# Linear attention with a gated product: q's last 64 tokens in float32r parts, attention in 288-column halves

## The chip, the core and the metric

The kernel runs on one core of a Trainium2 chip. The metric is device time in microseconds, from the start to the end of one execution. The engines are PE (TensorE, matmuls), DVE (VectorE), ACT (ScalarE), POOL (GpSimd) and SP (SyncE, which issues the DMAs here); each runs its own list of instructions in order and waits on semaphores for the others.

## The reference

Eight batches, eight heads, 576 tokens, 64 channels a head; q, k and v in float32. First linear attention, then a gated product:

```python
q_s = softmax(q over the 64 channels)            # exp(q - max), divided by sum + 1e-9
k_s = softmax(k over the 576 tokens)
kv = einsum('bhsd,bhse->bhde', k_s, v)           # 64 x 64 per head
x = einsum('bhsd,bhde->bhse', q_s, kv)           # then (batch, token, 512 channels)

gate = sigmoid(causal convolution of x over tokens, 5 taps, one weight per tap and channel)
val = x @ w_val                                  # 512 x 512
out = (gate * val) @ w_out                       # 512 x 512
```

The three weights arrive as float64. The kernel reads them as pairs of 32-bit words and builds float32 values of them on the chip.

## The kernel before, in words

**Layout.** From the attention on, everything is kept with channels on the partitions: a batch is four blocks of 128 channels (two heads each) by 576 tokens. Tokens are split into 512 "main" ones, in four groups of 128, and a tail of 64; the tails of an even and the following odd batch share one tile of 128 rows.

**Products in parts.** A float32 matmul runs as two instructions on PE, a high and a low pass. To avoid that, the two large products (`value` and `project`, by `split_product`, L528) split both sides into a float32r high part and a float32r rest, and add up three matmuls: low weight with high data, high with high, high with low. Each is done for the two halves of the 576 tokens, 288 columns, which lie in two PSUM banks side by side (`halved_bank`, L544). One `value` or `project` of a 128-channel block is so 4 x 3 x 2 = 24 matmuls.

**Attention** (`attend`, L481) takes one channel block of one batch. In batches 2 to 7 (not in `F32_BATCHES`, L25) it multiplies kv's parts (`kvs`, made by `kv_high` and `kv_low`) with q's parts for the 512 main tokens, three float32r matmuls of 512 columns, and then does the tail's 64 tokens with one float32 matmul from `kvd` (kv in float32) and `qTt` (the tail of q, turned). Batches 0 and 1 use float32 for all of it. q reaches this layout through PE: `q_turn` (L454) transposes eight 128 x 128 pieces into PSUM, `q_turned` copies them as the high part `qT`, `q_low` (L465, DVE) subtracts that from PSUM for the rest `qTlo`; `tail_turn` and `tail_turned` do the tail of two batches at once, in float32.

**After attention** x stays in PSUM while seven steps read it: `x_high` (a float32r copy, L497), `x_low` (the rest, DVE, L509), `first` (the last tap, L501), and four `tap`s (L513). A tap on DVE (`v`) is one multiply-add into the gate tile; a tap on ACT (`a`) writes a scaled copy `far`, which POOL then adds. Then `sigmoid` (ACT), `value` (PE), `gated` (DVE, value times gate), `g_high` (a float32r copy) and `g_low` (the rest, POOL or DVE), `project` (PE), `store` (a copy from PSUM and a DMA).

**Before it** come, per batch, for k: loads of a strided copy, `k_peak` (the maximum over tokens, DVE), `k_row` and `k_spread` (the row of maxima to DRAM and back, spread over the partitions), `k_sub` (five subtractions), `k_exp`; for q: `q_max`, `q_sub`, `q_exp`, `q_sum`, `q_mul`. Batches 0 and 1 have shorter ways through PE (`k_top`, `k_raise`, `k_turn`; for batch 0 `q_lift`, `q_peak`, `q_top`, `q_minus`, `q_raise`). The weights come in eight slabs (`load_words` 0 to 7; 8 is the convolution): `field`, `scaled`, `signed`, `part`, `joined` build a float32 value, `w_high` and `w_low` its parts.

**Order.** All of it stands in one list written out by hand, `ORDER` (L32 to L135), some 900 steps such as `tap 3 1 2 v`: batch 3, block 1, tap 2, on DVE. A letter chooses the engine (`a` ACT, `v` DVE, `p` POOL). Each engine does its own steps in the order of the list, and waits where the list puts a step ahead of its inputs.

**Buffers that the change touches.** PSUM has two buffers called "x" (attention, q's transposes, and the peaks and sums of the start) and two called "mm" (products, kv, the other transposes). The parts of x have six buffers each, `xh` and `xl`. One ring called `words`, four buffers of 4 KB a partition, holds the raw weight words, kv's parts and q's low parts. `qT` and `qTt` have one buffer each.

Of the kernel before, what the change touches and what calls it, by code (L numbers as in the profile page):

```python
# [24 lines left out]
F32_BATCHES = (0, 1)  # L25
# [17 lines left out]
    load_words 4, field 4, q_turned 0 0 a, signed 0, q_turned 0 1 a, scaled 2 a, q_sum 1, w_high 3 v, q_mul 0 4 p,
    joined 0 p, part 2 a, tail_turn 0, load_q 2, tail_turned 0 a, load_k 3, signed 2, attend 0 1, k_raise 1 2,
    first 0 1 a, x_high 0 1 a, load_v 1, field 5, tap 0 1 3 v, tap 0 1 2 v, tap 0 1 1 v, k_raise 1 0, joined 2 p,
    k_raise 1 3, attend 0 0, k_tail_turn 1, w_low 3 p, warm 8, first 0 0 a, x_low 0 1, x_high 0 0 a, tap 0 1 0 v,
    k_turn 1 0, w_high 0 a, k_tail_turned 1 a, tap 0 0 3 v, q_mul 1 3 p, x_low 0 0, scaled 5 a, k_turn 1 1,
    tap 0 0 2 v, load_v 4, tap 0 0 1 v, k_turned 1 0 a, part 4 a, q_mul 1 2 p, k_turned 1 1 a, scaled 4 a, attend 0 2,
    kv 1, q_mul 1 1 p, load_words 7, signed 4, w_low 0 p, first 0 2 a, tap 0 0 0 v, attend 0 3, part 5 a,
    load_words 6, x_high 0 2 a, sigmoid 0 0, tap 0 2 3 v, load_v 2, w_high 2 a, x_high 0 3 a, signed 5, x_low 0 2,  # L50
    first 0 3 a, kv_norm 1 a, joined 4 p, tap 0 2 2 v, joined 5 p, w_low 2 p, q_mul 1 0 p, x_low 0 3, load_km 2 1,
    w_high 4 a, tap 0 3 3 v, value 0 0, gated 0 0, tap 0 2 1 v, tap 0 3 2 v, field 7, w_low 4 p, w_high 5 a,
# [596 lines left out]
```

## Time and profile before

| | us |
|---|---|
| median of 3 runs (lowest to highest) | 320.44 (319.13 to 321.22) |
| the profiled execution | 321.3 |
| its span in the trace | 319.5 |

| engine | busy us of the span | share | instructions |
|---|---|---|---|
| PE, matmuls | 299.5 | 94% | 2553 |
| DVE | 268.2 | 84% | 363 |
| ACT | 203.4 | 64% | 315 |
| POOL | 187.8 | 59% | 156 |

Busy time of PE is modelled for pipelined matmuls: an instruction counts until its result has left the array, while the next has already begun, so start-to-start times are the safer measure of what a run of matmuls costs. An engine's idle time costs something only where it is on the way to the end. The mean granted TensorE clock was 0.998 of full speed. The `project` and `value` matmuls take 42% of the chain that ended last, attention's 4%.

### The profile page before, as it was taken

What the parts mean: (1) busy time and instruction counts of PE and PEld (TensorE: products, weight loads), DVE (VectorE), ACT (ScalarE), POOL (GpSimd) and SP (SyncE); (2) the same over time, 40 slices, a digit from 0 to 9 for tenths busy, and PEclk for the clock granted to TensorE, in tenths of its full rate; (3) what the DMA queues carried; (4) which work ended last, traced back from release to release, by engine and by line L of the source; (5) the groups of instructions that cost most, each with busy time, mean ns of one, the idle gap of its engine ahead of it and who ended that gap; (6) DMA issues with size and microseconds to landing.
All of it is one profiled execution on the core that took longest, in us unless ns stands there. A gap on an engine that the chain in (4) does not pass through costs nothing.

```text
span 319.5 us, 6403 instructions
## 1 busy us (share of the span) xinstructions
PE 299.5 (94%) x2553; PEld 276.4 (87%) x2553; DVE 268.2 (84%) x363; ACT 203.4 (64%) x315; POOL 187.8 (59%) x156
## 2 busy tenths in 40 slices
PE   2998689989899979999999999999999999999996
PEld 1347469988799969989999999999999999999995
DVE  3769999997897999799996979899899989868530
ACT  1579998665968499747983887569643773432200
POOL 2174467799867748858686776665758353311500
PEclk9999999999999999999999999999999999999999
DMA  7994897614798154663428178409300120012013
GB/s 247 376 388 153 301 400 272 201 37 147 237 248 312 50 172 174 193 249 98 147 56 327 42 242 260 182 0 353 99 0 25 50 77 0 2 74 76 0 39 111
DMA packets 20525, 51.25 MB, mean 160 GB/s; under 512 B 2832, under 2 KB 7312, under 8 KB 17808
## 3 DMA queue, kind: packets, MB, share of 16 engines
q1 hardware_dynamic: 20496, 50.85, 45.9%
q8 instruction: 20, 0.33, 0.5%
q14 instruction: 9, 0.07, 0.1%
HBM read 41.39 MB, written 9.45 MB: 159 GB/s over the span
## 4 chain that ended last, share of the span: by engine, by line
PE 60%; DMA 13%; ACT 12%; DVE 9%; issue 3%; POOL 2%; SPq 1%; DVEq 0%; POOLq 0%; ACTq 0%
PE val L535 21%; PE out L535 21%; DMA km<-in_k_strided 4%; PE kv L426 4%; PE x L491 4%; PE qTps L458 3%; DMA out<-o 2%; PE qlps L404 2%; DMA q<-in_q 2%; DVE gate L517 2%; PE qlps L409 2%; DMA kmax<-krow 2%; ACT far L520 2%; DVE kpk L273 2%; DMA ident<-in_ident 1%
## 5 line engine op out<-in xcount | busy, mean ns | idle before, releaser
L517 DVE SCALAR_TENSOR_TENSOR gate<-x,cw,gate 128x575 f32<-128x575 f32 (+3 forms) x99 | 78.1, 808 | 3.3 <-POOL gate L521 1.5
L521 POOL TENSOR_TENSOR gate<-gate,far 128x572 f32<-128x572 f32 (+3 forms) x29 | 39.6, 1369 | 39.0 <-ACT far L520 38.7
L535 PE MATMUL out<-gh,w_out_lo 128*128 128x288 f32 x256 | 56.9, 301 | 0.5 <-ACT gh L159 0.5
L535 PE MATMUL val<-xh,w_val_lo 128*128 128x288 f32 x256 | 56.5, 302 | 0.8 <-DVE o L161 0.7
L535 PE MATMUL out<-gl,w_out_hi 128*128 128x288 f32 x256 | 55.6, 296 | 0.9 <-DVE gl L564 0.9
L535 PE MATMUL val<-xl,w_val_hi 128*128 128x288 f32 x256 | 55.0, 296 | 0.8 <-DVE xl L511 0.8
L535 PE MATMUL out<-gh,w_out_hi 128*128 128x288 f32 x256 | 55.5, 295 | 0.0
L535 PE MATMUL val<-xh,w_val_hi 128*128 128x288 f32 x256 | 54.8, 295 | 0.0
L564 POOL TENSOR_TENSOR gl<-g,gh 128x576 fp32r<-128x576 f32 x25 | 36.5, 1463 | 30.5 <-ACT gh L159 23.3
L535 PEld LDWEIGHTS out<-gl,w_out_hi 128*128 128x128 f32 x256 | 41.4, 188 | 1.3 <-DVE gl L564 1.3
L535 PEld LDWEIGHTS val<-xh,w_val_lo 128*128 128x128 f32 x256 | 40.9, 188 | 1.6 <-DVE o L161 0.9
L535 PEld LDWEIGHTS val<-xl,w_val_hi 128*128 128x128 f32 x256 | 41.3, 188 | 1.0 <-DVE xl L511 1.0
L535 PEld LDWEIGHTS out<-gh,w_out_lo 128*128 128x128 f32 x256 | 41.2, 189 | 0.8 <-ACT gh L159 0.8
L535 PEld LDWEIGHTS out<-gh,w_out_hi 128*128 128x128 f32 x256 | 41.6, 188 | 0.0
L535 PEld LDWEIGHTS val<-xh,w_val_hi 128*128 128x128 f32 x256 | 41.3, 188 | 0.0
L382 POOL TENSOR_TENSOR q<-q,qs 128x512 f32<-128x512 f32 x25 | 26.2, 1068 | 16.3 <-DVE qs L362 16.3
L556 DVE TENSOR_TENSOR g<-val,gate 128x576 f32<-128x576 f32 x32 | 23.9, 751 | 9.8 <-PE val L535 6.9
L520 ACT ACTIVATE far<-x,cw 128x572 f32<-128x572 f32 (+3 forms) x29 | 21.0, 738 | 14.2 <-DVE gate L517 9.3
L159 ACT CAST gh<-g 128x576 fp32r<-128x576 f32 x25 | 16.8, 671 | 18.2 <-DVE g L556 18.2
L159 ACT COPY o<-out 128x576 f32<-128x576 f32 (+1 forms) x22 | 13.5, 617 | 21.9 <-PE out L535 12.1
L288 POOL TENSOR_TENSOR k<-k,kmax 128x512 f32<-128x512 f32 x18 | 25.0, 1402 | 1.3 <-DMA kmax<-krow 1.3
L524 ACT ACTIVATE gate<-gate 128x576 f32<-128x576 f32 x32 | 21.6, 685 | 6.0 <-DVE gate L517 3.5
(101 smaller groups left out, 588.0 us busy)
## 6 DMA issues: line engine op xcount, KB each, us to landing
out<-o SPq DMA_DIRECT2D x31, 288.0 KB, 2.3
...
```

What stands on the lines that cost most here:

```text
L159: nc.scalar.copy(out=out, in_=in_)
L288: engine(e).tensor_sub(kk[r, cs], kk[r, cs], mx[r, cs])
L382: engine(e).tensor_mul(qq, qq, s.unsqueeze(2).broadcast_to([P, H, D]))
L426: nc.tensor.matmul(acc[h * D:(h + 1) * D, p, :], T["k", b][:, c, cs] if c < 4 else ktz[b % 2][:, cs], T["v", b][:, c, hd] if c < 4 else T[ ...
L491: nc.tensor.matmul(ps[:, :MAIN], a, z, start=(i == 0), stop=(i == len(parts) - 1))
L517: nc.vector.scalar_tensor_tensor(out=a, in0=x, scalar=w, in1=a, op0=ALU.mult, op1=ALU.add)
L520: nc.scalar.activation(part, x, AF.Copy, scale=w)
L521: nc.gpsimd.tensor_add(a, a, part)
L524: nc.scalar.activation(T["gate", b, p], T["gate", b, p], AF.Sigmoid)
L535: nc.tensor.matmul(ps[:, cs], a[:, kb, ms], z[kb][:, cs], start=(kb == 0 and i == 0), stop=(kb == NB - 1 and i == 2),)
L556: nc.vector.tensor_mul(T["g", b, m], T["val", b, m], T["gate", b, m])
L564: engine(e).tensor_sub(T["gl", b, m], T["g", b, m], T["gh", b, m].bitcast(F32))
```

## The change

- Batch 1 leaves `F32_BATCHES`: its attention is done with parts, as batches 2 to 7 are. That adds `kv_high`, `kv_low` and two `q_low` for it.
- q's tail gets parts too. `qT` and `qTlo` grow from 512 to 576 columns a block; `tail_high` copies the batch's 64 tail columns of all four blocks from `qTt` into `qT` as float32r, `tail_low` subtracts that for two blocks at a time into `qTlo`. The float32 matmul of the tail goes.
- `attend` writes into a halved bank, and each of its matmuls is done for the two halves of 288 columns: six matmuls a step (four in batch 0, whose single float32 product is halved too).
- `xh` and `xl` become the two halves of one tile, six buffers called "pair". The weight words take buffers of the same ring. Kv's parts get a ring of their own with one buffer, q's low parts one with two.
- `ORDER` is new throughout, with other choices of engine.

```diff
-F32_BATCHES = (0, 1)
+F32_BATCHES = (0,)
...
+    def pair(name, dtype):
+        return work.tile([P, 2 * S], dtype, tag="pair", name=name, bufs=6)
...
-            T["words", i] = small.tile([P, n, 2], I32, tag="words", name=f"words{i}", bufs=4)
+            T["words", i] = pair(f"words{i}", I32)[:, :2 * C].rearrange("p (n t) -> p n t", t=2)
...
-        t = T["kvs", b] = small.tile([P, 2, C], F32R, tag="words", name=f"kvs_{b}", bufs=4)
+        t = T["kvs", b] = small.tile([P, 2, C], F32R, tag="kvs", name=f"kvs_{b}", bufs=1)
...
+    def q_across(b):
+        if ("qT", b) not in T:
+            T["qT", b] = work.tile([P, NB, S], F32 if b in F32_BATCHES else F32R, tag="qT", name=f"qT_{b}")
+        return T["qT", b]
...
+    def q_under(b, g):
+        if ("qTlo", b, g) not in T:
+            T["qTlo", b, g] = small.tile([P, 2, S], F32R, tag="qTlo", name=f"qTlo_{b}_{g}", bufs=2)
+        return T["qTlo", b, g]
...
+    def tail_high(b, e="p"):
+        copied(e, q_across(b)[:, :, MAIN:], T["qTt", b][:, :, rows(b)])
+
+    def tail_low(b, g, e="p"):
+        ps = slice(2 * g, 2 * g + 2)
+        engine(e).tensor_sub(q_under(b, g)[:, :, MAIN:], T["qTt", b][:, ps, rows(b)], T["qT", b][:, ps, MAIN:].bitcast(F32))
+
     def attend(b, p):
 
-        ps = bank(f"x_{b}_{p}", "x")
+        T["x", b, p] = halved_bank(f"x_{b}_{p}", "x")
...
         for i, (a, z) in enumerate(parts):
-            nc.tensor.matmul(ps[:, :MAIN], a, z, start=(i == 0), stop=(i == len(parts) - 1))
-        nc.tensor.matmul(ps[:, MAIN:S], kvd[b % 2][:, p], T["qTt", b][:, p, rows(b)], start=True, stop=True)
-        T["x", b, p] = ps[:, :S]
+            for cs in tokens("a"):
+                nc.tensor.matmul(T["x", b, p][:, cs], a, z[:, cs], start=(i == 0), stop=(i == len(parts) - 1))
...
-        xh = T["xh", b, p] = block("xh", f"xh_{b}_{p}", 6, F32R)
+        T["xx", b, p] = pair(f"x2_{b}_{p}", F32R)
+        xh = T["xh", b, p] = T["xx", b, p][:, :S]
...
-        xl = T["xl", b, p] = block("xl", f"xl_{b}_{p}", 6, F32R)
+        xl = T["xl", b, p] = T["xx", b, p][:, S:]
```

Of the new order, its beginning, and the places in batches 2, 3 and 4 that the prediction follows:

```diff
+    load_kc 0 1, load_q 0 0 2, k_top 0 1, load_kc 0 0, q_max 0 0 2, load_ident, q_peak 0 0 2, load_words 8, k_top 0 0,
+    load_words 1, field 1, q_top 0 0 2 a, scaled 1 v, load_q 0 2 5, field 8, signed 1, load_words 3, q_max 0 2 5,
+    load_kc 0 2, q_lift 0 0, k_raise 0 0, q_minus 0 0, load_kc 1 1, load_kc 0 3, q_peak 0 2 5, k_raise 0 1,
+    scaled 8 v, load_q 1, q_top 0 2 5 a, signed 8, field 3, part 3 v, k_top 1 1, part 1 p, scaled 3 a, k_top 0 2,
+    k_raise 1 1, warm 0, joined 1 p, warm 0, k_turn 0 0, load_kc 1 2, signed 3, q_raise 0 0, w_high 1 p, q_lift 0 1,
...
+    tap 2 1 1 v, k_sub 3 4 p, tap 2 1 0 v, project 1 1, k_sub 3 3 p, load_v 4, q_exp 3, q_sum 3, attend 2 2,
+    tap 2 0 1 a, q_mul 3 0 p, load_km 6 0, tap 2 0 0 a, x_high 2 2 v, k_peak 4 2, store 1 3 a, attend 2 3, load_q 4,
...
+    gated 2 0, q_sub 4 4 p, q_turned 3 0 v, g_high 2 1 a, value 2 2, kv_low 3 p, q_low 3 0, q_turned 3 1 a, q_low 3 1,
+    attend 3 0, value 2 3, x_high 3 0 a, first 3 0 a, q_sub 4 3 p, g_high 2 0 p, load_km 5 3, g_low 2 0 v,
+    g_low 2 1 p, gated 2 2, tap 3 0 3 v, k_peak 5 0, gated 2 3, g_high 2 2 p, x_low 3 0, g_high 2 3 v, load_km 5 2,
+    g_low 2 3 v, q_sub 4 1 p, load_q 5, g_low 2 2 p, k_sub 4 1 p, k_peak 5 2, q_sub 4 2 p, tail_low 3 1 p,
+    k_sub 4 0 p, attend 3 1, load_km 6 1, first 3 1 a, tap 3 0 2 a, tap 3 0 1 a, project 2 0, x_high 3 1 a,
...
+    q_turned 4 1 a, k_sub 5 3 v, k_peak 6 1, value 3 3, q_low 4 0, kv_low 4 v, tail_high 4 v, g_low 3 1 v, gated 3 2,
+    k_sub 5 1 p, k_peak 6 3, load_v 6, tail_low 4 0 v, g_low 3 0 p, q_low 4 1, attend 4 0, g_high 3 2 a, gated 3 3,
```

The steps of the old order that stand against the start:

```diff
-    load_kc 0 1, load_q 0 0 2, load_words 8, k_top 0 1, load_ident, q_lift 0 0, q_max 0 0 2, q_peak 0 0 2,
-    load_kc 0 0, k_top 0 0, load_words 1, load_kc 0 3, load_q 0 2 5, field 1, q_top 0 0 2 v, field 8, load_words 3,
-    q_minus 0 0, scaled 1 a, k_raise 0 1, k_top 0 3, part 1 a, k_raise 0 0, signed 1, load_kc 0 2, scaled 8 a,
-    q_max 0 2 5, load_kc 1 1, joined 1 p, field 3, load_q 1, q_raise 0 0, signed 8, load_words 0, k_turn 0 0,
...
-    part 3 a, w_low 1 p, k_turned 0 0 a, q_lift 0 1, q_top 0 2 5 a, q_minus 0 1, k_raise 1 1, signed 3, k_raise 0 2,
```

The steps whose engine changes, counted over both lists (before to after): tap on DVE 99 to 89, on ACT and POOL 29 to 39; g_high ACT 25 to 19, DVE 7 to 5, POOL 0 to 8; g_low POOL 25 to 16, DVE 7 to 16; q_sub POOL 22 to 26, DVE 5 to 1; q_mul POOL 25 to 28, DVE 7 to 3, ACT 4 to 5; w_high POOL 0 to 3; tail_high (new) ACT 3, DVE 1, POOL 4; tail_low (new) DVE 3, POOL 11; q_low DVE 12 to 14.

More of the change, by code (lines that the diff above doesn't have):

```diff
@@ L43 @@
[L43 to L52, printed above, removed]
@@ L68 @@
-    tap 1 3 0 v, g_low 1 1 v, sigmoid 1 2, value 1 2, gated 1 2, load_km 4 0, warm 0, tail_turn 2, kv_high 2 a,
-    q_turn 2 0, k_sub 3 0 v, k_peak 4 0, tail_turned 2 a, sigmoid 1 3, q_turn 2 1, load_v 3, q_turned 2 0 a,
-    g_low 1 0 p, g_high 1 2 a, q_turned 2 1 a, q_low 2 0, k_sub 3 4 p, load_q 3, kv_low 2 p, g_low 1 2 p, value 1 3,
-    attend 2 1, q_low 2 1, attend 2 0, x_high 2 1 a, gated 1 3, q_max 3, first 2 1 a, g_high 1 3 a, first 2 0 a,
-    k_sub 3 1 p, load_km 4 2, tap 2 0 3 v, x_low 2 1, tap 2 0 2 v, g_low 1 3 p, q_sub 3 3 p, q_sub 3 0 p, project 1 0,
@@ L93 @@
-    kv_high 4 v, value 3 2, q_turned 4 0 a, tail_turned 4 a, kv_low 4 p, value 3 3, q_sub 5 3 p, q_turned 4 1 a,
-    g_low 3 0 p, k_peak 6 1, sigmoid 3 3, q_low 4 0, gated 3 2, q_low 4 1, attend 4 0, gated 3 3, first 4 0 a,
-    attend 4 1, load_km 7 3, g_high 3 2 v, load_q 6, x_high 4 0 a, g_high 3 3 v, g_low 3 2 p, first 4 1 v, q_exp 5,
-    load_k 6, g_low 3 3 p, tap 4 1 3 a, tap 4 0 3 v, x_low 4 0, project 3 2, tap 4 1 2 a, tap 4 0 2 v, x_high 4 1 a,
-    project 3 1, tap 4 0 1 v, k_sub 5 2 p, tap 4 0 0 v, q_max 6, attend 4 2, x_low 4 1, k_peak 6 2, store 3 2 a,
@@ new lines @@
+    g_low 0 0 p, load_km 2 3, q_low 1 1, gated 0 2, q_low 1 0, kv_low 1 p, g_high 0 1 a, tail_low 1 0 p, g_high 0 2 a,
+    q_sub 2 1 p, g_low 0 2 v, field 6, gated 0 3, k_peak 2 0, part 7 a, attend 1 0, scaled 6 a, signed 6, first 1 0 a,
+    g_high 0 3 a, attend 1 1, g_low 0 3 v, g_low 0 1 p, k_peak 2 3, part 6 a, tap 1 0 3 v, project 0 0,
+    tail_low 1 1 p, q_sub 2 3 p, first 1 1 a, project 0 1, load_km 3 0, joined 7 p, joined 6 p, k_row 2, w_high 7 a,
+    x_high 1 1 a, w_high 6 p, x_high 1 0 a, store 0 0 a, tap 1 1 3 v, x_low 1 1, tap 1 0 2 v, w_low 6 p, tap 1 1 2 v,
@@ new lines @@
+    q_turned 5 0 v, kv_low 5 v, tail_low 5 0 v, q_turn 5 1, q_turned 5 1 a, value 4 3, q_low 5 0, q_low 5 1,
+    attend 5 1, gated 4 2, k_sub 6 3 v, tail_low 5 1 p, sigmoid 4 3, g_low 4 1 p, g_high 4 2 v, first 5 1 a,
+    load_km 7 3, attend 5 0, gated 4 3, g_high 4 3 a, first 5 0 a, tap 5 1 3 v, g_low 4 3 v, tap 5 0 3 v, g_low 4 2 p,
+    project 4 0, tap 5 0 2 v, project 4 1, tap 5 1 2 a, k_peak 7 3, tap 5 1 1 a, x_high 5 1 a, tap 5 1 0 a, x_low 5 1,
+    store 4 0 v, x_high 5 0 a, x_low 5 0, tap 5 0 1 v, sigmoid 5 1, q_sub 6 4 p, attend 5 3, first 5 3 a, project 4 2,
@@ new lines @@
+    value 5 2, q_sub 7 0 v, q_mul 6 0 a, kv_high 6 a, q_mul 6 3 p, g_high 5 1 p, tail_turn 6, q_turn 6 0, q_turn 6 1,
+    sigmoid 5 3, k_peak 7 2, q_turned 6 0 a, g_low 5 1 p, tail_turned 6 v, tail_high 6 p, kv_low 6 p, g_low 5 0 v,
+    q_turned 6 1 a, q_low 6 0, tail_low 6 0 p, q_sub 7 3 p, q_low 6 1, gated 5 2, tail_low 6 1 v, value 5 3,
+    attend 6 1, first 6 1 a, attend 6 0, k_row 7, g_high 5 2 p, gated 5 3, k_spread 7, tap 6 1 3 v, g_low 5 2 v,
+    g_high 5 3 a, x_high 6 0 a, g_low 5 3 v, first 6 0 v, tap 6 1 2 a, project 5 3, x_low 6 0, project 5 0,
```

167 lines of the change are left out of this document (82 added, 85 removed).

## The prediction

> **What bounds the kernel now.** I read the busy times by stretch first, cut where PE begins the first value product of batch 0 (47.4), of batch 2 (121.8), of batch 3 (154.3) and of batch 7 (290.6), and where it ends its last matmul (316.4). Columns: length, then busy time (count) of PE, weight loads, DVE, ACT, POOL, then clock, DMA share, GB/s.
> ```profile
> 0.00:47.40 47.40, 35.95 (x278) 21.58 (x278) 37.06 (x57) 35.05 (x65) 22.28 (x26) 1.00 0.85 310
> 47.40:121.80 74.40, 70.18 (x620) 65.93 (x618) 67.45 (x88) 55.54 (x93) 57.70 (x46) 1.00 0.59 193
> 121.80:154.30 32.50, 31.86 (x230) 30.64 (x229) 30.34 (x38) 24.18 (x39) 24.09 (x20) 1.00 0.49 164
> 154.30:290.60 136.30, 135.82 (x1243) 132.75 (x1242) 120.74 (x166) 83.55 (x114) 78.02 (x62) 1.00 0.32 113
> 290.60:316.40 25.80, 25.73 (x194) 25.49 (x192) 12.66 (x18) 4.75 (x9) 5.72 (x4) 1.00 0.11 41
> ...
> sum 319.50, PE 299.55 PEld 276.39 DVE 268.24 ACT 203.43 POOL 187.80; mean PE 49.92 PEld 46.07 DVE 44.71 ACT 33.91 POOL 31.30
> ```
> PE idles 11.4 us before 47.4, 4.2 in the second stretch, 0.6, 0.5 and 0.1 in the next three, so 5.4 us after 47.4. From 121.8 to the end PE is the bound; every matmul microsecond removed there should come off. Before 47.4 the chain changes from engine to engine. Between 47.4 and 121.8 PE and DVE (67.45 of 74.40) run neck and neck, and a DMA chain joins in, shown below.
>
> **The attention matmuls.** A busy PE overstates pipelined matmuls, so I take start-to-start times from the chain that ended last (start, length, what). Batch 7 first, then two runs of products for the unit price.
> ```profile
> 165.71 6.40 PE val L535 x48
> ...
> 274.20 0.70 PE x L491 x3
> 274.89 0.17 PE x L492 x2
> 275.06 0.74 PE x L491 x3
> 275.80 0.17 PE x L492 x2
> 275.97 6.46 PE out L535 x48
> ...
> 290.75 12.80 PE val L535 x96
> ```
> One 288-column float32r matmul costs 12.80 / 96 = 0.133 us. Two attention steps cost 275.97 - 274.20 = 1.77, and the product behind them is 0.06 longer than its like (6.46 against 6.40), which I put down to the return from float32: 1.83 a pair. After the change an attention step is six 288-column matmuls of the very form of the products: 6 x 0.133 = 0.80, 1.60 a pair. Gain 0.23 a pair, 0.115 a step; batches 2 to 7 have 24 steps: **-2.8 us**. The 64-column float32 matmuls go, two a step (one instruction each for the high and the low pass).
>
> The Trainium skill, "TensorE: Matmul & The Clock Gate", section "Back-to-back issue gap", speaks against this: it gives about 81 ns for a weight load with a 128-column matmul and 131 ns with 512 columns, a mostly fixed price. Interpolated, six at 102 ns would be 0.61 us where three at 131 and two at 81 or less were 0.55, so by that page the halves would lose 0.06 us a step, an estimate. This trace does not agree: 0.133 us at 288 columns and 0.70 / 3 = 0.233 at 512, in proportion to the columns.
>
> Batch 1 goes from float32 to parts. Its attention, in the timeline of PE:
> ```profile
> 62.45 1.02 PE L491 MATMUL x<-qT,kvd 128*128 128x512 f32 x2
> ...
> 63.48 1.08 PE L491 MATMUL x<-qT,kvd 128*128 128x512 f32 x2
> ...
> 64.53 0.51 PE L535 MATMUL out<-gh,w_out_lo 128*128 128x288 f32 x2
> ```
> A pair costs 64.53 - 62.45 = 2.08, with the same 0.06 2.14; after, 1.60. Two pairs: **-1.1**. Batch 0 keeps float32, in halves, four matmuls a step; 576 columns at the same price per column change it by under 0.1 us: 0. Together **-3.9 us** of PE work.
>
> **What the parts cost the other engines.** Rows by group (line, engine, operation, shapes, count | busy, mean ns | idle before):
> ```profile
> L517 DVE SCALAR_TENSOR_TENSOR gate<-x,cw,gate 128x575 f32<-128x575 f32 (+3 forms) x99 | 78.1, 808 | 3.3 <-POOL gate L521 1.5 <-ACT xh L159 0.5 <-ACT gate L505 0.2
> L521 POOL TENSOR_TENSOR gate<-gate,far 128x572 f32<-128x572 f32 (+3 forms) x29 | 39.6, 1369 | 39.0 <-ACT far L520 38.7
> L564 POOL TENSOR_TENSOR gl<-g,gh 128x576 fp32r<-128x576 f32 x25 | 36.5, 1463 | 30.5 <-ACT gh L159 23.3 <-DVE gh L161 7.2
> L288 POOL TENSOR_TENSOR k<-k,kmax 128x512 f32<-128x512 f32 x18 | 25.0, 1402 | 1.3 <-DMA kmax<-krow 1.3
> L556 DVE TENSOR_TENSOR g<-val,gate 128x576 f32<-128x576 f32 x32 | 23.9, 751 | 9.8 <-PE val L535 6.9 <-ACT gate L524 1.4 <-POOL q L349 1.3
> L349 POOL TENSOR_TENSOR q<-q,qm 128x512 f32<-128x512 f32 x22 | 23.3, 1073 | 3.4 <-DVE qm L345 3.4
> L468 DVE TENSOR_TENSOR qTlo<-qTps,qT 128x1024 fp32r<-128x1024 f32 x12 | 14.4, 1217 | 0.6 <-ACT qT L159 0.5
> L524 ACT ACT_TABLE_LOAD x8 | 10.3, 1283 | 0.9 <-DVE gate L517 0.7
> L564 DVE TENSOR_TENSOR gl<-g,gh 128x576 fp32r<-128x576 f32 x7 | 7.0, 1007 | 0.1
> ...
> L253 POOL TENSOR_TENSOR f<-e,f 128x512 int32<-128x512 int32 x8 | 11.1, 1385 | 18.6 <-DVE e L249 14.7 <-ACT xh L159 1.5 <-ACT w_val_hi L159 1.2
> ...
> L253 POOL TENSOR_TENSOR cw<-e,f 128x20 int32<-128x20 int32 x1 | 0.2, 226 | 0.4 <-ACT f L165 0.4
> ```
> I counted the steps of both orders by engine. **DVE**: 10 taps go (-8.1), 9 subtractions of g come (+9.1), 2 of batch 1's q_low (+2.4); of the rest 14 leave and 15 come, of like lengths, which I call even. Net +3.4, about +1.3% of its busy time. **POOL**: 10 tap additions (+13.7), 9 subtractions of g less (-13.2), 4 q_sub and 3 q_mul more (1.07 each, +7.5), and work this trace doesn't show there: 8 copies of g, 3 of weights, 4 tail_high, 11 tail_low. The two L253 rows give 2.36 ns a column, so a 128-column tail_low is 0.48 and a 256-column tail_high 0.78; a copy of g or of weights lies between 0.23 (the shortest row) and 1.46 (the subtraction of that size); I take the middle, 0.85. That is 5.3 + 3.1 + 9.4, and with single steps some **+28 us** (bounds +21 to +35). **ACT**: its 10 more taps replace copies of like size; the new order goes to and fro between exponential and sigmoid 19 times, not 15: 4 table loads, +5.1.
>
> What hides this: POOL idles 132 us of the span, ACT 116, so they cost 0, as long as no matmul waits for the instruction in question; a tap on ACT and POOL lasts 2.1 us where one on DVE lasts 0.8, and what is behind a waiting POOL instruction waits too. DVE's cover is thin only between 47.4 and 121.8: 7 us of idle. Counted by means, its steps from batch 0's first value to batch 2's go from 68.2 to 70.9, while PE's fall from 68.1 to 66.5. I take 0 for it and keep +2.5 as its upper bound.
>
> **New waits.** Attend now needs tail_low, mostly on POOL, and engines take their steps in the order listed. At one place that costs PE time. Between value 2 2 and attend 3 1 (batch 2's third product, batch 3's second attention) PE has attend 3 0 and value 2 3 to do, 0.80 + 3.20 = 4.0 us. POOL has, from the end of value 2 2 on: g_high 2 2, which needs gated 2 2 on DVE, then q_sub 4 1, g_low 2 2, k_sub 4 1, q_sub 4 2, and only then tail_low 3 1. By the rows, 0.75 + 0.85 + 1.07 + 1.46 + 1.40 + 1.07 + 0.48 = 7.1 us. So PE stands 3.1 us before attend 3 1, and project 2 0 is queued behind it. The stretch's present idle of 0.6 falls into it, I take it: **+2.5 us**. Bounds: +1.9 with the shortest copy; and if POOL is busy without a break from kv_low 3 on, as the listing suggests (q_sub 4 3, g_high 2 0 and g_low 2 1 stand in between, and gated 2 2 stands behind a g_low 2 0 that waits for POOL), PE loses 2.3 us more: +4.8. Elsewhere I found the tail's parts at most a us or two late, and take 0: between value 3 3 and attend 4 0 DVE has 5.0 us listed against PE's 3.2.
>
> Tail_high must wait for the last attend of the batch before, since qT has one buffer; it stands behind it: 0. One buffer for kv's parts and two for q's low parts are no wait either: kv_high and q_low of a batch stand behind the last attend of the batch before. The x tile shared by both parts is released by the same products as before: 0. The weight words now share the ring of x tiles: x parts of batch 0 wait for the part and signed steps of words 1, 3, 4 and 5, which stand ahead of them: 0.
>
> **The start.** Up to value 0 0 the order is new throughout. Rows of the chain, then of ACT and DVE:
> ```profile
> 14.40 1.90 PE kps L317 x8
> 16.30 0.64 PE qpk L388 x3
> 16.94 2.29 PE qlps L404 x4
> ```
> ```profile
> L310 ACT ACTIVATE kc<-kc,ktop 128x576 f32<-128x576 f32 x8 | 5.9, 773 | 0.0
> L165 ACT ACTIVATE e<-e 128x512 f32<-128x512 f32 x7 | 4.4, 633 | 3.0 <-DVE e L239 3.0
> L413 ACT ACTIVATE q<-qlps 128x1024 f32<-128x1024 f32 x2 | 2.0, 1023 | 4.6 <-PE qlps L409 4.6
> ```
> ```profile
> 17.33 0.46 ACT L159 COPY qtop<-qpk 8x384 f32<-8x384 f32 x1
> ...
> 49.58 0.75 DVE L511 TENSOR_TENSOR xl<-x,xh 128x576 fp32r<-128x576 f32 x1
> ```
> The identity now follows a 288 KB load in place of a 20 KB one (about 0.9 us at 310 GB/s), but the peaks are turned before q is lifted, so the copy of the peaks no longer holds PE between: even, so the first subtraction still ends at 14.4. Then PE turns three peaks (0.64, to 15.0) and ACT does q_top 0 2 5, scaled 3, k_raise 1 1 and only then q_raise 0 0: 0.46 + 0.63 + 0.77 + 1.02 = 2.9, to 17.9. q_lift 0 1 needs that PSUM bank and started at 16.94. So +1.0, which passes to the last q_raise and the sum on DVE. From there to the last xl of batch 0 (ends at 50.3) DVE's steps add up to the same in both orders (25.8 and 25.9 us), and PE's value 0 0 ends on it. **+1.0 us**, bounds -1 (the new interleaving gains on DVE) and +2.5 (q's fourth part on POOL is late, behind the new steps there).
>
> **The q chain of batch 3**, which ends in PE's longest wait after 47.4:
> ```profile
> 97.44 6.94 DMA q<-in_q
> 104.41 2.29 DVE qm L345
> ...
> 113.25 0.72 ACT far L520
> ```
> ```profile
> PE x L491 <- ACT far L520: 1.8, 1, 1.8
> ```
> The load of q waits for the turn of batch 2's q, then q_max, subtractions, q_exp and a far tap that must read x before attend 2 3 may overwrite it. The new order has the same chain, with two far taps behind q_exp where one was (+0.7), but attend 2 2 is moved in front of the wait (0.8 of PE work, which then fills it). 0.
>
> **Sum.** -2.8 - 1.1 + 2.5 + 1.0 = **-0.4 us**. The profiled run took 321.3 (span 319.5 and 1.8 around it), 0.9 above the median of 320.44; so 320.9 beside it, and **320.0 us** as a median. A measurement of this kernel tells about 1% (3.2 us) from no change: 317.2 and 323.6 are the lines.
>
> **Rivals.**
> 1. *Faster: the order closes gaps.* The start does not lose its 1.0, and of the 4.2 us that PE idles between 47.4 and 121.8 three quarters go: 320.0 - 4.2 = 315.8. For it: 10 taps leave DVE, whose taps and x parts are what attention waits for there, and every other term is -3.9. Against: the causes of the gaps, q's load and DVE's load, are still there. Chance 0.34.
> 2. *Slower: the tail's parts come late at both places.* POOL is full from kv_low 3 on (+2.3), and attend 4 0 waits for tail_low 4 0 on DVE, which stands behind q_low, kv_low, tail_high, a g_low, gated 3 2 and a k_peak: 5.0 - 3.2, +1.8. 320.0 + 4.1 = 324.1. It decides from the point where POOL or DVE has no gap left in the 8 us before attend. For it: by my count POOL's work from batch 2's value to batch 3's is 30 us against PE's 30.5, and DVE's is 34 against 33.5 in the next batch. Against: in the runs of batches 5 to 7 there is slack. Chance 0.16.
> 3. *DVE becomes the bound between 47.4 and 121.8*, and the 1.6 us that PE saves there is lost: 321.6. For it: DVE's count exceeds PE's there now. Against: it idled 7 us. Chance 0.13.
> 4. *The change doesn't shorten attention*, since each half loads its weights again. The load's own row:
> ```profile
> L535 PEld LDWEIGHTS val<-xh,w_val_hi 128*128 128x128 f32 x256 | 41.3, 188 | 0.0
> ```
> Were that not hidden, 28 steps at 6 x 0.188 = 1.13 cost 320.0 + 28 x 0.33 = 329.2. Against it stand the 96 products in 12.80. The Trainium skill's section named above would make it a mechanism of every short matmul; the rows of this case don't bear it out. Chance 0.02.
>
> The forecast itself has 0.35 (318 to 322). So faster 0.34; slower 0.16 + 0.02 = 0.18; same 0.35 + 0.13 = 0.48. The range holds the forecast, the third rival, most of the first and half of the second, with the start's and the wait's bounds: 314.0 to 324.0.
>
> **What would show it.** Right: attention as six matmuls, pairs 1.6 us apart start to start; in batches 1 to 7 no float32 matmul but kv and transposes; a first value at about 48.4; a wait of PE of some 3 us before attend 3 1, with POOL's tail part of q as releaser; POOL near 216 us, DVE near 271. Wrong: attention above 0.85 us a step; no wait at attend 3 1, or one of 5; PE idle after the first value below 4 us or above 11; a start off by more than 2.5 us.

## The result, and the profile after

The changed kernel took 317.64 us (median of 20 runs, 315.61 to 320.07) against 320.32 (317.75 to 323.5) for the kernel before: ratio 0.9929, 95% interval 0.9902 to 0.9955. Two later series on other occasions gave 0.9976 (0.9948 to 1.0005) and 0.9939 (0.9906 to 0.9973). The forecast of 320.0 was 2.4 us too high: over the three series the change saves some 0.5%, less than the 1% that the forecast set as the line, but a gain, as two of the three intervals lie wholly below 1. The profiled execution took 316.62, its span is 314.8.

Busy time by stretch in the changed kernel, cut at the same events as before: first value product of batches 0, 2, 3 and 7, end of the last matmul. Columns: length, busy time (count) of PE, weight loads, DVE, ACT, POOL, then clock, DMA share, GB/s.

```profile
0.00:47.95 47.95, 31.96 (x261) 19.63 (x262) 40.79 (x60) 32.94 (x55) 27.31 (x32) 0.96 0.80 288
47.95:118.75 70.80, 68.15 (x630) 66.53 (x628) 67.45 (x88) 54.26 (x86) 59.95 (x54) 1.00 0.64 219
118.75:151.10 32.35, 31.18 (x237) 30.70 (x234) 31.80 (x34) 21.55 (x28) 29.68 (x27) 1.00 0.59 191
151.10:285.90 134.80, 134.16 (x1259) 132.78 (x1258) 122.75 (x169) 92.29 (x137) 86.41 (x78) 1.00 0.31 106
285.90:311.60 25.70, 25.69 (x193) 25.45 (x192) 10.57 (x16) 6.52 (x10) 8.87 (x7) 1.00 0.11 41
sum 311.60, PE 291.14 PEld 275.10 DVE 273.35 ACT 207.55 POOL 212.22; mean PE 58.23 PEld 55.02 DVE 54.67 ACT 41.51 POOL 42.44
```

Against the rows of before: the start is 0.6 us longer, the second stretch 3.6 shorter, the third and fourth together 1.7 shorter, the last alike. In the second stretch DVE does exactly the work it did before (67.45) in 70.80 us instead of 74.40.

The chain that ended last, for the attention of batches 5 and 7 and the products behind it (start, length, what):

```profile
203.23 1.59 PE x L513 x12
204.82 6.39 PE out L556 x48
...
270.06 1.59 PE x L513 x12
271.65 9.60 PE out L556 x72
```

Two attention steps take 1.59 us, as forecast (1.60), and the two products behind them 6.39, without the 0.06 that they cost on top before.

What PE waited for (total us, times, longest):

```profile
...
PE x L513 <- DVE gate L538: 3.2, 1, 3.2
...
PE out L556 <- DVE gl L585: 1.6, 2, 1.2
...
PE x L513 <- ACT far L541: 0.7, 1, 0.7
PE x L513 <- DVE qTlo L482: 0.6, 1, 0.6
```

No row has POOL's `qTlo` as releaser: the wait of some 3 us before `attend 3 1`, the largest positive term of the sum, is not there; that was one of the forecast's own signs of being wrong. The queue in front of it was there. PE, then POOL:

```profile
134.19 0.69 PE L513 MATMUL x<-qT,kvs 128*128 128x288 f32 x4
134.72 0.43 PE L513 MATMUL x<-qTlo,kvs 128*128 128x288 f32 x2
```
```profile
139.36 0.46 POOL L500 TENSOR_TENSOR qTlo<-qTt,qT 128x128 fp32r<-128x128 f32 x1
```

POOL ended `tail_low 3 1` at 139.8, 5.6 us after `attend 3 1` had begun and 9.6 us after PE had ended `value 2 2` (130.2), where the forecast had 7.1 us and, with POOL busy without a break, 9.4. PE did not wait because it did not need it: `attend b p` reads half `p // 2` of q's low part, so `attend 3 1` reads half 0, which `tail_low 3 0` had filled by 122.4. Half 1 is read by `attend 3 2` and `attend 3 3`, the pair at 146.2.

### The profile page after: what moved, and what is told of

The parts are those of the page before. It is cut to its first block, busy times and chain, and to the rows that moved or that the text cites. A ratio compares the mean times of both kernels' runs of the same rounds, so it can differ in the third digit from the quotient of the medians.

```text
span 314.8 us, 6475 instructions
## 1 busy us (share of the span) xinstructions
PE 291.1 (92%) x2569; PEld 275.1 (87%) x2569; DVE 273.4 (87%) x365; ACT 208.0 (66%) x315; POOL 212.2 (67%) x195
## 4 chain that ended last, share of the span: by engine, by line
PE 63%; DVE 22%; ACT 4%; DMA 4%; issue 4%; POOL 2%; SPq 0%; DVEq 0%; ACTq 0%
PE out L556 24%; PE val L556 22%; PE x L513 6%; PE kv L433 5%; DVE gate L538 4%; DVE qm L352 3%; DVE qTlo L482 2%; PE qlps L411 2%; PE qTps L465 2%; DVE kpk L280 2%; PE qlps L416 2%; DVE qs L367 2%; DVE gl L585 2%; DVE g L577 2%; DMA q<-in_q 1%
## 5 line engine op out<-in xcount | busy, mean ns | idle before, releaser
L556 PE MATMUL val<-x,w_val_hi 128*128 128x288 f32 x512 | 88.9, 295 | 0.0
L538 DVE SCALAR_TENSOR_TENSOR gate<-x,cw,gate 128x575 f32<-128x575 f32 (+3 forms) x89 | 70.2, 806 | 8.1 <-POOL gate L542 3.8
L556 PEld LDWEIGHTS val<-x,w_val_hi 128*128 128x128 f32 x512 | 75.4, 188 | 0.0
L542 POOL TENSOR_TENSOR gate<-gate,far 128x572 f32<-128x572 f32 (+3 forms) x39 | 51.5, 1322 | 34.0 <-ACT far L541 33.3
L556 PE MATMUL val<-x,w_val_lo 128*128 128x288 f32 x256 | 56.7, 303 | 1.2 <-ACT o L166 0.6
L556 PEld LDWEIGHTS val<-x,w_val_lo 128*128 128x128 f32 x256 | 40.9, 188 | 2.5 <-ACT o L166 0.9
L541 ACT ACTIVATE far<-x,cw 128x572 f32<-128x572 f32 (+3 forms) x39 | 27.9, 741 | 15.2 <-DVE gate L538 9.9
L585 POOL TENSOR_TENSOR gl<-g,gh 128x576 fp32r<-128x576 f32 x16 | 23.6, 1473 | 11.9 <-DVE gh L168 7.8
L526 ACT ACTIVATE gate<-x,cw 128x576 f32<-128x576 f32 x24 | 17.8, 745 | 18.7 <-PE x L513 17.2
L577 DVE TENSOR_TENSOR g<-val,gate 128x576 f32<-128x576 f32 x32 | 23.9, 747 | 7.0 <-PE val L556 2.8
L356 POOL TENSOR_TENSOR q<-q,qm 128x512 f32<-128x512 f32 x26 | 28.4, 1106 | 0.5 <-PE val L556 0.4
L295 POOL TENSOR_TENSOR k<-k,kmax 128x512 f32<-128x512 f32 x18 | 23.9, 1338 | 0.2
L532 DVE TENSOR_TENSOR x<-x,x 128x576 fp32r<-128x576 f32 x32 | 23.6, 748 | 0.5 <-ACT gate L526 0.2
```

The costliest lines, as they stand in the source:

```text
L295: engine(e).tensor_sub(kk[r, cs], kk[r, cs], mx[r, cs])
L356: engine(e).tensor_sub(qq, qq, T["qm", b][:, cs].unsqueeze(2).broadcast_to([P, H, D]))
L532: nc.vector.tensor_sub(xl, T["x", b, p], T["xh", b, p].bitcast(F32))
L538: nc.vector.scalar_tensor_tensor(out=a, in0=x, scalar=w, in1=a, op0=ALU.mult, op1=ALU.add)
L541: nc.scalar.activation(part, x, AF.Copy, scale=w)
L542: nc.gpsimd.tensor_add(a, a, part)
```

## The experiments

My first theory, A: the attention's matmuls bring the gain, at the forecast's price, and no wait takes it back. Its rival, B: the new order brings it. Each was tried alone, beside a second series of the changed kernel. All times are medians; "before" was 319.51 us in this series, 319.90 and 320.03 in the two after it.

**The changed kernel again.** 

> The changed kernel itself once more, beside the other three on the same chip. Both theories: 0.993 of the time of before (0.990 to 0.996), a span near 316, the first value product at about 48 us and the last matmul 263.7 us behind it. If its first value and its stretches come out elsewhere than in the first profile (47.95, then 70.8, 32.3, 134.9 and 25.6 us), the difference is what one profile of this kernel varies by.

Measured: 317.95 us, ratio 0.9976 (0.9948 to 1.0005).

**Old order, new attention.** The changed code with the list of steps of before, into which the new steps were put where their inputs are first there, on POOL:

```diff
-    g_low 1 0 p, g_high 1 2 a, q_turned 2 1 a, q_low 2 0, k_sub 3 4 p, load_q 3, kv_low 2 p, g_low 1 2 p, value 1 3,
-    attend 2 1, q_low 2 1, attend 2 0, x_high 2 1 a, gated 1 3, q_max 3, first 2 1 a, g_high 1 3 a, first 2 0 a,
...
+    tail_high 2 p, sigmoid 1 3, q_turn 2 1, load_v 3, q_turned 2 0 a, g_low 1 0 p, g_high 1 2 a, q_turned 2 1 a,
+    q_low 2 0, tail_low 2 0 p, k_sub 3 4 p, load_q 3, kv_low 2 p, g_low 1 2 p, value 1 3, attend 2 1, q_low 2 1,
+    tail_low 2 1 p, attend 2 0, x_high 2 1 a, gated 1 3, q_max 3, first 2 1 a, g_high 1 3 a, first 2 0 a, k_sub 3 1 p,
```

> The attention of the change (parts for the tail, halves, batch 1 in parts, the new tiles) in the order of before; the new steps are put behind the q_turned, q_low, tail_turned or kv_norm that they belong to, tail parts on POOL. Theory A (the matmuls of attention bring the gain, the order little): PE's work is 3.9 us shorter, of which 1.6 lies in the stretch from batch 0's first value to batch 2's, where DVE and the load of q hold PE as well; so 316.5 to 318.5 us against 320.3, ratio 0.988 to 0.994. Theory B (the order brings the gain, by fewer waits of PE): the shorter matmuls only lengthen the waits, and the added steps of POOL and DVE cost what is left; 319.5 to 321.5 us, ratio 0.997 to 1.004.

Measured: 323.78 us, ratio 1.0141 (1.0101 to 1.0181). Both theories miss: the same matmuls that were to save 1% cost 1.4% here. What PE waited for:

```profile
PE x L513 <- POOL qT L168: 2.2, 1, 2.2
PE x L513 <- POOL kvs L459: 2.0, 1, 2.0
PE x L513 <- POOL qTlo L500: 1.9, 1, 1.9
```

Three waits of about 2 us for POOL: for the tail's copy (in batch 0, ahead of the first value), for `kv_low 2`, which is no new step but has new ones ahead of it, and for a tail's rest (in the last third). POOL's timeline up to `kv_low 2`, and PE's at the wait for a rest:

```profile
98.31 0.87 POOL L168 CAST qT<-qTt 128x256 fp32r<-128x256 f32 x1 [2.33 <-ACT qTt L166]
99.15 1.44 POOL L585 TENSOR_TENSOR gl<-g,gh 128x576 fp32r<-128x576 f32 x1
100.54 0.46 POOL L500 TENSOR_TENSOR qTlo<-qTt,qT 128x128 fp32r<-128x128 f32 x1
...
102.44 1.26 POOL L459 TENSOR_TENSOR kvs<-kvd,kvs 128x512 fp32r<-128x512 f32 x1
```
```profile
241.69 0.29 PE L513 MATMUL x<-qTlo,kvs 128*128 128x288 f32 x1
243.88 0.40 PE L513 MATMUL x<-qTlo,kvs 128*128 128x288 f32 x1 [1.89 <-POOL qTlo L500]
```

POOL stands 2.3 us before batch 2's copy of the tail, since ACT turns the tail's PSUM over late, and everything behind it, `kv_low 2` among it, is late too. At 241.7 the first half of the columns could go; the second, which holds the tail, could not. That is the mechanism forecast for `attend 3 1`, at another place of another order.

**New order, old attention.** The changed order and tiles with the attention of before (512 columns of parts and a float32 tail, batch 1 in float32); the steps for the parts that this leaves unused are left out.

```diff
-F32_BATCHES = (0,)
+F32_BATCHES = (0, 1)
...
-            for cs in tokens("a"):
-                nc.tensor.matmul(T["x", b, p][:, cs], a, z[:, cs], start=(i == 0), stop=(i == len(parts) - 1))
...
+            nc.tensor.matmul(ps[:, :MAIN], a, z, start=(i == 0), stop=(i == len(parts) - 1))
+        nc.tensor.matmul(ps[:, MAIN:S], kvd[b % 2][:, p], T["qTt", b][:, p, rows(b)], start=True, stop=True)
```

> The order and the tiles of the change, with the attention of before: 512 main columns in one matmul each, the tail's 64 in float32, batches 0 and 1 in float32; the steps for the tail's parts and for batch 1's parts are left out. Theory A: without the shorter matmuls the order gives 0 to 1 us back, 319.3 to 321.3 us, ratio 0.997 to 1.003; attention steps cost 1.83 a pair. Theory B: 316.5 to 318.5 us, ratio 0.988 to 0.994, and PE's idle time behind the first value is below the 5.4 us of before.

Measured: 320.85 us, ratio 1.0035 (0.9995 to 1.0074), within A's range. By the medians the order alone saves nothing, and the new attention costs 4.3 us in the old order and saves 2.9 us (320.85 to 317.95) in the new one. The trace splits this otherwise. Its windows from the first value of batch 0 to that of batch 2, and from batch 3's to batch 7's:

```profile
51.50:121.60 70.10, 69.18 (x620) 65.67 (x618) 64.80 (x85) 53.46 (x84) 55.94 (x47) 1.00 0.66 222
...
154.15:290.30 136.15, 135.79 (x1242) 132.53 (x1241) 121.93 (x164) 91.91 (x135) 82.11 (x70) 1.00 0.31 105
```

Behind the first value PE idles 2.2 us, not the 5.4 of before: B's other sign came true. From the first value to the end of the last matmul this kernel takes 264.6 us, the one before 269.0, the changed one 263.1 to 264.0 in three executions. So behind the first value the order alone saves 4.4 us, 4.3 of them in the second stretch, and the new attention adds only 0.6 to 1.5. What B got wrong is the start: the first value comes at 51.5, 4.1 us later than before. Part of that is the order's, as shown further down. Part is there ahead of any attention step: the transposes of k's tail in batch 0 (`k_tail_turn 0`) begin at 23.9, against 19.7 to 22.0 in seven executions of the new order with halves, since the same matmuls ahead of them run slowly for longer. Whether that belongs to this kernel or to the execution isn't shown, and with it how much of the 2.9 us is attention's.

**512 and 64 columns.** The changed kernel, with each of attention's matmuls cut into 512 and 64 columns instead of two halves:

```diff
-            for cs in tokens("a"):
+            for cs in (slice(0, MAIN), slice(MAIN, S)):
```

> As the change, but each of the attention matmuls takes 512 and 64 columns in place of twice 288 (all in parts, no float32 in batches 1 to 7). By the price per column (theory A): 3 x (0.235 + 0.030) = 0.80 us a step, as with the halves, and the time of the changed kernel within 0.3 us. If a weight load bounds a short matmul (the rival of the prediction), a 64-column matmul costs far more than 0.030: with the 0.068 that a 64-column float32 instruction took before, 0.90 a step, 28 steps +3 us, so 320 to 321; with a whole weight load of 0.188, 1.27 a step and +13 us.

Measured: 322.74 us, ratio 1.0121 (1.0074 to 1.0169), 4.8 us over the changed kernel beside it. The price per column on which theory A rested does not hold for a short matmul. Its chain:

```profile
243.66 1.98 PE x L513 x12
245.64 6.47 PE out L556 x48
...
256.32 0.95 PE x L513 x6
257.27 3.27 PE out L556 x24
```

A pair costs 1.98, and the product behind it 3.27 instead of 3.20: together 2.05 for two steps. Three matmuls of 512 columns at the forecast's 0.233 are 0.70, so the three of 64 cost (1.025 - 0.70) / 3 = 0.11 us each, against 0.03 in proportion to their columns. The surcharge of 0.07 on the next product, which I had put down to the return from float32, is there with no float32 in attention. The Trainium skill, "TensorE: Matmul & The Clock Gate", section "Back-to-back issue gap", states that at 128 columns the weight load counts too, so that a matmul takes about 81 ns where its columns alone would take about 56. The trace agrees with it in kind (0.11 us at 64 columns), while at 288 and 512 columns (0.133 and 0.233 us) the price still goes by the columns.

**PE busy early.** The first values of the traces of all kernels here lie between 45.7 and 51.7 us, and the runs of the changed kernel up to 4.5 us apart. In the first 20 us the same matmuls take twice as long in some rows as in others; in the changed kernel's trace:

```profile
7.12 3.62 PE L411 MATMUL qlps<-q,ident 128*128 128x512 f32 x4
...
14.20 1.88 PE L411 MATMUL qlps<-q,ident 128*128 128x512 f32 x4
```

Theory C was that PE, had it been at work before, would not start at half rate. Five matmuls on zeros go ahead of the first step:

```diff
+        early = bank("early")
+        for i in range(5):
+            nc.tensor.matmul(early[:, :256], kvd[0][:, 0], kvd[0][:, 1:3], start=True, stop=True)
         for step in ORDER:
```

> The changed kernel with five matmuls of zeros (128x256 float32, into a bank of their own) ahead of the first step, so that PE is at work from about 2 us instead of 6.7 us. Theory C (the spread of the runs, 315.6 to 320.2 us, and the different first values of the traces, 47.9 to 51.7 us, come from how long PE's early matmuls run at half rate; being busy earlier ends that sooner): the early groups of four identity matmuls take 2.0 us instead of 3.3 to 3.8 from the first or second group on, the first value lies at 45 to 47 us, the lowest and highest run are under 3 us apart, the median 315 to 317 us. Rival (the slow phase does not depend on what PE did before): first value 48 to 51.5 us, spread over 4 us, median 317 to 319 us.

> The same five early matmuls in the kernel before. Theory C: spread under 3 us, median 1 to 3 us below the kernel before (317 to 319 us); and against the changed kernel with the same early matmuls the difference of the two medians shows the change without the luck of the start: 2.9 us by the terms of the prediction without its wait, 0.4 by its whole sum, 4.7 by the spans of the two profiled executions. Rival: as the kernel before.

Measured: 316.57 us (315.16 to 319.04) with the changed kernel, 320.10 (317.45 to 327.21) with the one before. The first median lies in C's range, but the spread stays (3.9 and 9.8 us, not under 3), the first values are 47.6 and 46.8, and the first group is as slow as ever:

```profile
1.29 4.63 PE L624 MATMUL early<-kvd 128*128 128x256 f32 x10 [1.29 <-POOL kvd L619]
...
7.14 3.62 PE L411 MATMUL qlps<-q,ident 128*128 128x512 f32 x4
```

C falls: 4.6 us of matmuls on zeros ahead did not end the slow phase. A second series of the changed kernel with early matmuls, beside one without:

> The changed kernel with the five early matmuls of zeros, beside the changed kernel in one call. If they help: 0.7 to 1.5 us below it (as 316.57 against 317.64 and 317.95). Rival (they do nothing, as the rows of the identity matmuls say, which still took 3.6 us in the first group of four): within 0.5 us.

Measured: 317.35, beside 316.76 without them: no gain is left.

**Blocks 1 and 2 of batch 3 exchanged**, in the steps `attend`, `first`, `x_high`, `x_low`, `tap` and `sigmoid`, so that the step at 134 us does read half 1:

```diff
-    k_sub 4 0 p, attend 3 1, load_km 6 1, first 3 1 a, tap 3 0 2 a, tap 3 0 1 a, project 2 0, x_high 3 1 a,
+    k_sub 4 0 p, attend 3 2, load_km 6 1, first 3 2 a, tap 3 0 2 a, tap 3 0 1 a, project 2 0, x_high 3 2 a,
```

> The changed kernel with blocks 1 and 2 of batch 3 exchanged in the steps of x, so that the attention step at about 134 us is one of the second half, whose subtraction of the tail POOL ends at about 139.8 us. This is the case that the prediction computed for attend 3 1 by mistake. Its queue arithmetic: PE waits 3 to 5.6 us at that step, released by POOL's subtraction, and the time rises by 2.5 us (the price in the prediction's sum) to 5.5 us over the changed kernel: 320 to 323.5 us. Rival (a wait of that size is made good afterwards, because the steps behind it find their inputs ready): PE waits, but the time rises by less than 1 us.

Measured: 323.55 us, ratio 1.0093 (1.0052 to 1.0133), 5.6 to 6.8 us over the changed kernel's three medians, a little more than the price expected. The wait and what follows it:

```profile
134.01 0.30 PE L513 MATMUL x<-qTlo,kvs 128*128 128x288 f32 x1
139.06 0.61 PE L513 MATMUL x<-qTlo,kvs 128*128 128x288 f32 x1 [4.76 <-POOL qTlo L500]
139.47 0.68 PE L556 MATMUL out<-gh,w_out_lo 128*128 128x288 f32 x2
139.95 0.68 PE L556 MATMUL out<-gh,w_out_hi 128*128 128x288 f32 x2
...
144.27 0.44 PE L556 MATMUL out<-gh,w_out_hi 128*128 128x288 f32 x2
144.55 0.43 PE L556 MATMUL out<-gl,w_out_hi 128*128 128x288 f32 x2
```

PE waits 4.76 us, between the forecast's 3.1 for that queue and the 5.4 of its upper case (3.1 + 2.3). On top of it the next products start 0.48 us apart by twos until 144.3, where the rest of the kernel has 0.27. The windows of that place show the granted clock (the first number behind the busy times):

```profile
...
139.00:141.00 2.00, 1.94 (x8) 1.94 (x9) 0.02 (x1) 1.29 (x3) 1.25 (x2) 0.50 0.00 0
...
143.00:145.00 2.00, 2.00 (x13) 2.00 (x12) 2.00 (x3) 0.00 (x0) 2.00 (x3) 0.68 0.00 0
```

The clock falls to 0.50 for some 5 us after the wait. Ten groups of two at 0.21 us more each are 2.1 us: this wait cost 4.8 + 2.1 us. The stretch from batch 2's first value to batch 3's grew from 32.3 to 37.9, by 5.6: of that price only the 1.2 us of idle that were there before are saved, and nothing is made good later. The Trainium skill, "TensorE: Matmul & The Clock Gate", section "HAM oscillation — how this bites in real kernels", states that PE should not idle for more than about 3.4 us. The traces agree only in part: behind the waits of 1.9 and 2.0 us in the old order the clock stays at 1.00, and behind the one of 3.2 us before `attend 0 2` in the changed kernel it is at 0.54; but behind the one of 2.25 us in batch 0 of the old order it is at 0.56 too. Windows of the changed kernel, then of the old order with the new attention:

```profile
41.80:44.00 2.20, 2.15 (x6) 1.11 (x6) 2.17 (x4) 0.38 (x1) 0.84 (x2) 0.54 0.56 220
```
```profile
33.70:36.70 3.00, 2.93 (x6) 1.62 (x6) 2.86 (x8) 2.04 (x5) 0.44 (x1) 0.56 1.04 418
```

So those two waits, too, cost more than their own length, and the length alone doesn't tell which waits do.

**Old order, tail parts unread.** The old-order kernel computes its tail parts at the same places into a tile that nobody reads:

```diff
-        copied(e, q_across(b)[:, :, MAIN:], T["qTt", b][:, :, rows(b)])
+        T["aside", b] = work.tile([P, NB, 2 * (S - MAIN)], F32R, tag="aside", name=f"aside_{b}", bufs=1)
+        copied(e, T["aside", b][:, :, :S - MAIN], T["qTt", b][:, :, rows(b)])
...
-                nc.tensor.matmul(T["x", b, p][:, cs], a, z[:, cs], start=(i == 0), stop=(i == len(parts) - 1))
+                nc.tensor.matmul(T["x", b, p][:, cs], a, z[:, min(cs.start, MAIN - HALF):min(cs.stop, MAIN)], start=(i == 0), stop=(i == len(parts) - 1))
```

> The kernel with the old order and the new attention, with its tail parts computed by the same instructions at the same places, but into a tile that nobody reads; the second halves of the attention's matmuls take columns 224 to 511 instead of 288 to 575, so that the last 64 tokens' attention is left out of the result. Same matmuls, same POOL work, no wait for a tail part. Theory A2 (the old order loses with the new attention because attention waits for POOL's tail parts, 2.2 and 1.9 us in its trace): 4 us less than the 323.8 us with the waits, 319 to 320.5 us, ratio 0.997 to 1.003. Rival A3 (the loss lies in the stretch before 122 us, where batch 1's parts and steps wait for other things, and POOL's load): 322.5 to 324, ratio above 1.009.

Measured: 321.36 us, ratio 1.0062 (1.0027 to 1.0097), 2.4 us less than with the waits: between the two theories. Of the windows, the second stretch and that from batch 3's value to batch 7's, first with the waits, then without:

```profile
46.20:122.85 76.65, 69.72 (x630) 66.76 (x628) 69.10 (x91) 56.94 (x94) 60.26 (x53) 1.00 0.58 183
...
155.80:292.90 137.10, 134.67 (x1259) 132.87 (x1258) 119.98 (x166) 83.62 (x114) 83.93 (x74) 1.00 0.32 112
```
```profile
45.70:122.10 76.40, 69.46 (x630) 66.73 (x628) 68.55 (x92) 56.77 (x93) 60.29 (x53) 1.00 0.56 184
...
154.95:289.80 134.85, 134.50 (x1259) 132.82 (x1258) 121.01 (x165) 83.57 (x114) 84.23 (x74) 1.00 0.32 114
```

The late stretch falls by 2.25 us, nearly the whole of the 2.4; the early one stays at 76.4, where before had 74.40. So the tail's waits explain the loss late. Early, the parts are still in POOL's queue, read or not, and the wait of 2.0 us for `kv_low 2` behind them stays.

**Old order, no parts for batch 1.** The kernel with unread tail parts, its batch 1 back in float32:

```diff
-F32_BATCHES = (0,)
+F32_BATCHES = (0, 1)
```

`kv_high 1`, `kv_low 1`, the two `q_low 1` and the two `tail_low 1` leave the list of steps.

> The old order with unread tail parts (the last 64 tokens' attention of batches 0 to 7 is left out of the result, as columns 224 to 511 are taken in place of 288 to 575), and batch 1's attention in float32 without its parts. Theory A4 (batch 1's parts, pressed into the old order, are what is left of the loss: 2.0 us of wait for POOL's part of kv and the load on ACT and DVE before 122 us): 2.3 us below the kernel with unread tail parts, 318.5 to 319.5 us, and the stretch from the first value of batch 0 to that of batch 2 falls from 76.4 to 74 us; with the matmuls of batches 2 to 7 at the prediction's price even 316.7 to 318. Rival A5 (the stretch is long for another reason, such as x's banks or the shared tile of x's parts): 320.5 to 322, stretch over 75.5.

Measured: 319.47 us, ratio 1.0019 (0.9979 to 1.0059), 1.9 us less again; the early stretch is 75.20 us, a little over the 74 that A4 wanted. A4's price holds (1.9 for 2.3), its place only by half: the wait of 2.0 us that it named is still there, and the traces show it to be batch 2's. With both costs gone the old order is back where the kernel before was: its late stretch has the gain of attention (134.60 us by its windows, before 136.30), its early stretch is 0.8 longer.

**The changed kernel, batch 1 in float32**, in halves, without the six steps that make its parts, beside a third series of the changed kernel:

```diff
-F32_BATCHES = (0,)
+F32_BATCHES = (0, 1)
```

> The changed kernel once more, as the measure for the three others of this call. Theory (attention's matmuls at the prediction's price, and no wait in their place): 316.5 to 318 us, ratio to the kernel before 0.991 to 0.997. Rival (the whole sum of the prediction, -0.4): ratio 0.998 to 1.001.

> The changed kernel with batch 1's attention in float32, in halves of 288 columns like batch 0's, and without the steps that make its parts. Theory by the prediction's term for batch 1 (2.08 us a pair against 1.58, two pairs, -1.1 us): 1 us more than the changed kernel, 318 to 319 us, and the stretch from the first value of batch 0 to that of batch 2 is 1 us longer than 70.8. Rival (PE idles 2.0 to 3.0 us in that stretch and the parts of batch 1 cost the other engines more than they save PE): within 0.3 us of the changed kernel or below it, the stretch 70.8 or shorter.

Measured: 316.76 us for the changed kernel (ratio 0.9939, 0.9906 to 0.9973) and 316.84 for batch 1 in float32 (0.9962, 0.9927 to 0.9998). The windows of the latter, second stretch:

```profile
49.20:119.20 70.00, 68.79 (x623) 66.45 (x621) 64.17 (x85) 53.73 (x85) 56.91 (x51) 1.00 0.66 221
```

Float32 gives PE 0.6 us more to do than the 68.15 of the changed kernel and takes 3.3 us from DVE's 67.45: the stretch is 70.0 instead of 70.8. Batch 1's parts buy nothing. And one pair of batch 1 in float32 halves:

```profile
64.17 2.10 PE L512 MATMUL x<-qT,kvd 128*128 128x288 f32 x8
65.90 0.64 PE L555 MATMUL out<-gh,w_out_lo 128*128 128x288 f32 x2
```

65.90 - 64.17 = 1.73 us, where 512 and 64 columns had taken 2.08: 70% of what batch 1 gained on PE comes from the halves, not from the parts.

No version tried beats the changed kernel by more than the runs scatter.

## Why the prediction was right in kind and wrong in a step

**The step that failed: "PE stands 3.1 us before attend 3 1 ... I take it: +2.5 us".** The queue was as long as in the forecast's upper case, but the dependence was misread: the step reads the half of q's low part that `p // 2` selects, half 0, and `tail_low 3 1` makes half 1. The trace of the changed kernel has no such wait; with the blocks exchanged it appears, at 4.76 us. Without this term the sum is -0.4 - 2.5 = -2.9 us, so 317.5 as a median; the three series gave 317.64, 317.95 and 316.76.

**That this number fits is partly luck**, as the other terms show:

| term | forecast, us | measured, us | from |
|---|---|---|---|
| attention, batches 3 to 7 (20 of the 24 steps) | -2.3 | -1.7 | from batch 2's first value to batch 7's, 168.8 before, 167.1 after: PE's work -2.3, its idle +0.7 |
| attention, batches 1 and 2 | -1.6 | 0 to +1 | second stretch in the new order: 70.1 with the old attention; 70.8, 71.1, 70.2 with the new |
| wait at attend 3 1 | +2.5 | 0 | no such wait |
| start | +1.0 | +0.6 to +1.4 | first value 47.4 before; 47.9, 48.8, 48.1 in three executions after |
| second stretch, by the order | 0 | -4.3 | 74.4 before; 70.1 with the old attention in the new order |

Attention was priced rightly (1.59 a pair; forecast 1.60), and most of it came off where PE is the bound. The idle that grew there by 0.7 us is for a `g_low`, a far tap and a `q_low` (the rows of `gl`, `far` and `qTlo` above), not for a part of the tail: those were taken at 0 with reason.

**The second stretch** is where rival 1 was right: the order closed gaps there, which the forecast had put at 0 on a count of DVE's steps (68.2 to 70.9). DVE's busy time came out the same as before, 67.45, and its idle time went from 7.0 to 3.4 us. PE's idle fell from 4.2 us to between 2.1 and 3.0 in three executions, and to 0.9 with the old attention in the new order, by rival 1's three quarters. One gap has a name: the wait of 1.8 us for a far tap of batch 2, which the forecast kept, is in the second stretch of neither of these kernels. The three versions in the new order that carry 68.15, 68.79 and 69.18 us of PE work there all need 70.0 to 71.1 us of it: what attention saves PE there, from either batch, is worth nothing. Why the new order packs DVE better isn't isolated to single steps.

**The start** came out at the forecast's size, but not by its way. `q_lift 0 1` was to stand until `q_raise 0 0` ended at 17.9; in the changed kernel it began at 14.20 (the second row shown under "PE busy early"), ahead of that step on ACT, so it did not wait for it:

```profile
15.80 1.00 ACT L420 ACTIVATE q<-qlps 128x1024 f32<-128x1024 f32 x1
```

Two larger differences nearly cancel. `k_tail_turn 0` began at 20.0 to 21.5 in three executions of the changed kernel, at 23.2 and 22.6 in two of the one before. From there to the first value PE took 27.3 to 27.9 us in all nine executions in the new order and 24.0 to 24.5 in all five in the old one, 3.4 more. The forecast had taken DVE's steps there as equal. Some took longer: a step of `signed`, one of `q_mul` and one of `field`, in the changed kernel, and then the last two forms before:

```profile
25.16 1.41 DVE L256 SCALAR_TENSOR_TENSOR e<-words,e 128x512 int32<-128x512 int32 x1
26.49 1.53 DVE L389 TENSOR_TENSOR q<-q,qs 128x512 f32<-128x512 f32 x1
27.94 1.26 DVE L246 TENSOR_SCALAR e<-words 128x512 f32<-128x512 f32 x1
```
```profile
27.31 0.36 DVE L239 TENSOR_SCALAR e<-words 128x512 f32<-128x512 f32 x1
...
28.25 0.89 DVE L382 TENSOR_TENSOR q<-q,qs 128x512 f32<-128x512 f32 x1
```

A step of `signed` (the first row) took 0.69 before. PE's wait for DVE before `attend 0 2` is 3.2 us now, and was 0.3. Why these steps take longer, no run isolates.

Rival 2's mechanism is real: it is what the old order shows, and what exchanging two blocks makes. In the changed order no attention step meets it. `tail_low 4 0` was not waited for either: the 0.6 us in batch 4 are for `q_low`. Rival 3 did not decide: DVE is busy for 95% of the second stretch, but the stretch got shorter, and with 3.3 us less of DVE's work (batch 1 in float32) it is only 0.8 shorter still. Rival 4 is refuted for halves (0.133 us each); a price that doesn't shrink with the columns shows only at 64.

**Sizes on the other engines.** A copy of g on POOL was taken at 0.85 and took 0.68, `tail_high` at 0.78 and took 0.51, `tail_low` at 0.48 and took 0.51; so POOL came to 212.2 us, not 216, and DVE to 273.4, not 271. None of PE's waits in the changed kernel is put down to one of these steps on POOL.

**What stays open.** The spans of the two profiled executions differ by 4.7 us, the medians by 1.6 to 3.3. The execution profiled before took 321.3, 1 to 2 us above its medians, and those profiled after 316.2 to 317.8, at or below theirs. What differs between executions of one kernel is at least how long PE runs at half rate in the first 20 us; what ends that phase was not found, nor why the new order's start takes 3.4 us more behind it.
